# Sums of four v tokens by an accumulating load instead of TensorE, in a new instruction list with the stores on SyncE

## The chip, the cores and the metric

One core of a Trainium2 chip. The time is device time in microseconds (us) from the core's first to its last work, as the median of several executions. Executions of one kernel agree within 1 to 2%; a run more than 1.5% above the fastest of its kernel is called slow and left out of the ratios. In a trace, PE is TensorE, DVE is VectorE, ACT is ScalarE, POOL is GpSimd and SP is SyncE; a `q` behind a name is that engine's DMA issue. "L359" is a line of the kernel that the trace belongs to, so the same statement has another number in each kernel.

## The reference, cut to what matters

```python
# q, k, v: (8 batches, 8 heads, 576 tokens, 64), float32
q_d = q.reshape(B, H, 144, 4, D).mean(axis=3)      # means of 4 tokens
k_d = k.reshape(B, H, 144, 4, D).mean(axis=3)
v_d = v.reshape(B, H, 144, 4, D).mean(axis=3)
out_up = np.repeat(softmax_attention(q_d, k_d, v_d), 4, axis=2)
out_local = softmax_attention_within_3_tokens(q, k, v)     # banded mask
x = (out_up + out_local).transpose(0, 2, 1, 3).reshape(4608, 512)
out = elu(x @ w_in) @ w_out                                # 512 -> 2048 -> 512
```

The change touches only how `v_d` is formed for batches 3 to 7.

## The kernel before

The kernel handles heads in pairs (`j` = 0 to 3) and the tokens of the second part in nine blocks of 512. All instructions of all engines stand in one long list of words, `ORDER`, which was tuned; each engine executes its own instructions in the order of the list. `Cv3.0` is the cast of v of batch 3, pair 0 to fp16, `VD3.0` the copy of its four-token means out of PSUM, `mm1.2.5` one 128-row piece of the first matrix product for block 2, and `e`, `m`, `g` are the three steps of the ELU that TensorE's second product needs.

```python
def vsum_mm(b, j, to):                   # means of 4 tokens, by TensorE
    v16 = stV[(b, j)][0]
    for c in range(NB):                  # NB = 6
        nc.tensor.matmul(
            to[0:KG, c // 3, :],
            at_once("VR")[:, 48 - 24 * (c % 3) : 120 - 24 * (c % 3)], v16[:, c, :, :],
            start=(c % 3 == 0), stop=(c % 3 == 2),
        )

def turn(n, b, j):                       # words Tq, Tk
    ...
    if n == "q":
        vsum_mm(b, j, to[:, :, GW : GW + 128])

def v_away(b, j):                        # word VD
    x = tp[("v", b, j)] if nines(b) else tp[("q", b, j)][:, :, GW : GW + 128]
    vd = sb.tile([KG, 2, 128], FP16, tag="vd", bufs=7, name="vd")
    nc.vector.tensor_copy(out=vd[:], in_=x[0:KG])          # PSUM -> SBUF

def cast_v(b, j):                        # word Cv; cast_qk is alike
    nc.gpsimd.tensor_copy(out=t[:], in_=st32.pop(("v", b, j)).rearrange(...))

def x_add(b, j, t):                      # word X: local + global part, on GpSimd
    eng = nc.vector if (b, j, t) in X_DVE else nc.gpsimd
    eng.tensor_tensor(out=xts[t][...], in0=ln[:, a:z], in1=_rep4(...), op=AB.add)

def masked(b, j):                        # word M: two SBUF inputs
    nc.vector.tensor_tensor(out=mex[:], in0=pex[:], in1=mk2, op=AB.mult)

def elu_min(t, fc):                      # word m: SBUF to SBUF, fp16
    nc.vector.tensor_scalar(out=e[:], in0=e[:], scalar1=1.0, scalar2=-1.0, op0=AB.min, op1=AB.add)

def elu_add(t, fc):                      # word g: reads PSUM; TensorE waits for gt
    nc.vector.scalar_tensor_tensor(out=gts[t][:, fc, :], in0=hps[(t, fc)][:], scalar=0.0,
                                   op0=AB.max, in1=els.pop((t, fc))[:], op1=AB.add)

def store(t, tt):
    nc.scalar.dma_start(out=out[r : r + 128, :], in_=oss.pop((t, tt))[:])
```

The softmax here doesn't subtract the row's maximum and nothing guards it: scores larger than these inputs give would overflow.

Of the kernel before, what the change touches and what calls it, by code (L numbers as in the profile page):

```python
# [36 lines left out]
X_DVE, K_DVE = ((0, 3, 0),), ((0, 0), (0, 1))  # L37
ORDER = """
KM Lq0.0 KV TBL Lk0.0 FILL Lq0.1 KN Lk0.1 KE Lq0.2 KI Lk0.2 Cq0.0 Ck0.0 Lq0.3 Tq0.0 Lk0.3 Aq0.0
Tk0.0 Cq0.1 Lv0.0 Ak0.0 Ck0.1 Lv0.1 Z1 Tq0.1 Fq0.0 Lv0.2 SL0.0 Cq0.2 Aq0.1 Lv0.3 Fk0.0 Ck0.2  # L40
Tk0.1 G00.0 Z1 Tq0.2 Ak0.1 Cq0.3 G10.0 Fq0.1 Aq0.2 SD0.0 Ck0.3 Tk0.2 H00.0 Fk0.1 H10.0 KS Ak0.2
M0.0 SL0.1 Z2 Tq0.3 G00.1 Fq0.2 Cv0.0 G10.1 Fk0.2 Aq0.3 SD0.1 M0.1 Tk0.3 H00.1 H10.1 Fq0.3 Cv0.1
Ak0.3 SL0.2 Z1 VS0.0 Dq1.0 Fk0.3 G00.2 G10.2 VD0.0 WI0 SD0.2 WI1 Z2 VS0.1 H00.2 H10.2 Cv0.2
SL0.3 VD0.1 M0.2 G00.3 Z3 VS0.2 G10.3 Dk1.0 M0.3 SD0.3 OUT0.0 H00.3 VD0.2 WI2 H10.3 LG0.0 Z1
DEN0 WI3 WLv1.0 OUT0.1 Cv0.3 Lv1.0 RC0 Lv1.1 LG0.1 Lv1.2 VS0.3 RB0.0 Lv1.3 VD0.3 MUL0.0 RB0.1 Z1
OUT0.2 MUL0.1 X0.0.0 OUT0.3 LG0.2 X0.0.1 LG0.3 RB0.2 X0.1.1 X0.1.0 MUL0.2 Z1 RB0.3 Q0 MUL0.3
X0.2.1 X0.2.0 Q1 X0.3.0 Dk1.1 Q2 Dq1.1 mm1.0.0 mm1.0.2 e.0.0 X0.3.1 Tq1.1 WO0 Tk1.1 e.0.2 m.0.0
mm1.0.1 g.0.0 Ak1.1 WO1 mm1.0.3 Aq1.1 m.0.2 mm1.0.6 Fk1.1 WO2 e.0.3 Fq1.1 e.0.1 Tq1.0 Dk2.0
Tk1.0 Aq1.0 m.0.3 m.0.1 Ak1.0 g.0.1 WO3 SC1.1 Fq1.0 WLv2.0 Dq2.0 Lv2.0 mm1.0.7 Fk1.0 E01.1 Lv2.1
Cv1.0 Lv2.2 g.0.3 E11.1 Lv2.3 g.0.2 VS1.0 Lq3.0 mm1.0.11 VD1.0 e.0.7 M1.1 mm1.0.13 e.0.6 m.0.7  # L50
e.0.11 g.0.7 SC1.0 m.0.6 e.0.13 mm1.0.5 m.0.11 g.0.11 E01.0 m.0.13 mm1.0.9 E11.0 g.0.13 g.0.6
Tq1.2 Tk1.2 M1.0 Aq1.2 mm1.0.14 Ak1.2 Lk3.0 Cv1.1 Fq1.2 OUT1.0 e.0.5 Fk1.2 mm1.0.4 e.0.9 m.0.5
LG1.0 g.0.5 Tq1.3 e.0.4 Dq2.1 m.0.9 VS1.1 g.0.9 Aq1.3 mm2.0.0 VD1.1 e.0.14 Fq1.3 Tk1.3 OUT1.1
Ak1.3 Dk2.1 m.0.4 g.0.4 LG1.1 Fk1.3 SC1.2 m.0.14 g.0.14 mm2.0.1 E01.2 mm1.0.12 E11.2 mm1.0.8
e.0.12 M1.2 SC1.3 Lv3.0 m.0.12 e.0.8 g.0.12 Cv1.2 E01.3 m.0.8 mm1.0.10 g.0.8 E11.3 VS1.2 e.0.10
mm1.0.15 M1.3 VD1.2 DEN1 e.0.15 m.0.10 g.0.10 OUT1.2 m.0.15 mm2.0.2 RC1 LG1.2 g.0.15 RB1.1 RB1.0
MUL1.1 mm2.0.3 MUL1.0 X1.1.1 RB1.2 oc.0.0 MUL1.2 X1.0.2 mm2.0.4 X1.1.2 X1.0.1 Tq2.1 st.0.0 Tk2.1
Aq2.1 Cv1.3 mm2.0.5 Ak2.1 Fq2.1 X1.2.1 VS1.3 Fk2.1 Tq2.2 X1.2.2 mm2.0.6 Aq2.2 VD1.3 OUT1.3 Fq2.2
RB1.3 LG1.3 mm2.0.7 MUL1.3 Tk2.2 oc.0.1 mm2.0.8 Cv2.0 Lq3.1 Ak2.2 mm2.0.9 X1.3.2 Fk2.2 X1.3.1
mm2.0.10 st.0.1 Cv2.1 mm2.0.11 VS2.0 oc.0.2 mm2.0.12 Cv2.2 Lk3.1 VD2.0 SC2.1 mm2.0.13 E02.1  # L60
mm2.0.14 E12.1 Cv2.3 Lv3.1 mm2.0.15 M2.1 Tq2.0 oc.0.3 Cq3.0 Lq3.2 Tk2.0 Aq2.0 mm1.1.0 Ak2.0
Fq2.0 mm1.1.2 e.1.0 Ck3.0 Lk3.2 Fk2.0 SC2.2 e.1.2 m.1.0 g.1.0 E02.2 m.1.2 mm1.1.4 Lv3.2 g.1.2
Cv3.0 E12.2 Lq3.3 Tq2.3 e.1.4 M2.2 mm1.1.1 Aq2.3 Lk3.3 m.1.4 VS2.3 st.0.3 g.1.4 Cq3.1 Tk2.3
e.1.1 VD2.3 mm1.1.3 Ak2.3 m.1.1 Lv3.3 g.1.1 Ck3.1 SC2.0 e.1.3 Fk2.3 mm1.1.7 E02.0 m.1.3 g.1.3
E12.0 VS2.2 Fq2.3 Cv3.1 Lq4.0 mm1.1.5 e.1.7 VD2.2 M2.0 SC2.3 e.1.5 m.1.7 mm2.1.0 Lk4.0 E02.3
g.1.7 m.1.5 E12.3 mm1.1.6 g.1.5 Lv4.0 VS2.1 M2.3 e.1.6 mm1.1.8 VD2.1 m.1.6 DEN2 e.1.8 g.1.6
Cv3.2 Lq4.1 OUT2.1 RC2 mm1.1.9 LG2.1 m.1.8 g.1.8 RB2.1 st.0.2 OUT2.3 e.1.9 MUL2.1 mm1.1.10 LG2.3
m.1.9 RB2.3 g.1.9 X2.1.3 e.1.10 OUT2.0 X2.1.2 MUL2.3 mm1.1.11 LG2.0 m.1.10 RB2.0 g.1.10 X2.3.2
e.1.11 mm2.1.1 MUL2.0 Cv3.3 mm1.1.12 m.1.11 g.1.11 X2.0.3 OUT2.2 e.1.12 X2.0.2 RB2.2 LG2.2
mm1.1.14 m.1.12 g.1.12 X2.3.3 Tq3.0 e.1.14 MUL2.2 mm1.1.13 Aq3.0 Cq3.2 Tk3.0 m.1.14 e.1.13 Lk4.1  # L70
mm2.1.2 VD3.0 X2.2.2 Ak3.0 g.1.14 Tq3.2 Ck3.2 KD3.0 mm1.1.15 m.1.13 Aq3.2 Lv4.1 g.1.13 Cv4.0
Lq4.2 Tk3.2 e.1.15 VD3.2 X2.2.3 mm1.2.0 Ak3.2 m.1.15 g.1.15 Tq3.1 e.2.0 KD3.2 mm2.1.3 Aq3.1
Cq3.3 Tk3.1 m.2.0 oc.1.0 Lk4.2 mm1.2.2 VD3.1 Cq4.1 Ak3.1 g.2.0 Ck4.0 mm2.1.4 st.1.0 KD3.1 e.2.2
Ck3.3 SC3.1 mm1.2.12 m.2.2 E03.1 Lv4.2 g.2.2 Cv4.1 Lq4.3 mm2.1.5 E13.1 mm1.2.1 e.2.12 M3.1 SC3.0
m.2.12 e.2.1 g.2.12 mm2.1.6 E03.0 m.2.1 g.2.1 mm1.2.10 E13.0 Cv4.2 Tq3.3 e.2.10 Tk3.3 M3.0 Aq3.3
mm1.2.15 m.2.10 Ak3.3 g.2.10 Cq4.0 mm2.1.7 e.2.15 VD3.3 Lk4.3 KD3.3 mm2.1.8 m.2.15 oc.1.1 Lv4.3
g.2.15 st.1.1 SC3.3 Lq5.0 Lk5.0 mm2.1.9 E03.3 mm2.1.10 E13.3 mm1.2.5 M3.3 SC3.2 e.2.5 mm1.2.6
E03.2 m.2.5 g.2.5 mm2.1.11 E13.2 Tq4.0 e.2.6 M3.2 oc.1.2 Tk4.0 m.2.6 mm2.1.12 st.1.2 g.2.6 Ck4.2
Ak4.0 DEN3 Aq4.0 Ck4.1 KD4.0 mm2.1.13 VD4.0 Lv5.0 RC3 Lq5.1 mm2.1.14 SO3 mm2.1.15 Tq4.1 oc.1.3
Tk4.1 st.1.3 Cq4.2 mm1.2.3 Aq4.1 Cq5.0 Ak4.1 Lk5.1 mm1.2.7 VD4.1 Lv5.1 e.2.3 KD4.1 Tq4.2 Lq5.2  # L80
e.2.7 m.2.3 g.2.3 Tk4.2 SI3 Cq4.3 mm2.2.0 m.2.7 g.2.7 Ck4.3 Aq4.2 Lk5.2 mm1.2.9 Ak4.2 Ck5.0
VD4.2 Lv5.2 mm1.2.4 e.2.9 KD4.2 m.2.9 SC4.2 e.2.4 g.2.9 E04.2 m.2.4 mm1.2.11 g.2.4 E14.2
mm1.2.13 e.2.11 M4.2 SC4.1 e.2.13 m.2.11 mm2.2.1 g.2.11 E04.1 m.2.13 mm1.2.8 E14.1 g.2.13
mm1.2.14 e.2.8 M4.1 m.2.8 SC4.0 e.2.14 g.2.8 E04.0 m.2.14 mm2.2.2 g.2.14 E14.0 OUT3.0 mm2.2.3
MUL3.0 Cv4.3 OUT3.1 oc.2.0 M4.0 Lq5.3 OUT3.3 st.2.0 Lk5.3 MUL3.1 X3.0.3 mm2.2.4 Lv5.3 X3.0.4
MUL3.3 mm2.2.5 X3.1.3 mm2.2.6 X3.3.4 X3.1.4 OUT3.2 X3.3.3 Tq4.3 MUL3.2 Cv5.1 mm2.2.7 Aq4.3
X3.2.3 Tk4.3 VD4.3 oc.2.1 mm2.2.8 Ck5.2 Ak4.3 mm1.3.0 st.2.1 X3.2.4 KD4.3 Cv5.0 SC4.3 e.3.0
mm1.3.3 Cv5.2 E04.3 Lq6.0 m.3.0 mm2.2.9 E14.3 g.3.0 Tq5.0 e.3.3 M4.3 mm1.3.7 Aq5.0 m.3.3 g.3.3
Cq5.1 DEN4 e.3.7 VD5.0 Cq5.3 Lk6.0 mm1.3.6 RC4 m.3.7 Tk5.0 SO4 g.3.7 Tq5.1 e.3.6 Ck5.1 Ak5.0
mm1.3.5 m.3.6 Aq5.1 Lv6.0 g.3.6 Cq5.2 mm2.2.10 Lq6.1 e.3.5 KD5.0 VD5.1 Lk6.1 mm1.3.1 m.3.5 Lv6.1  # L90
g.3.5 Lq6.2 Tk5.1 e.3.1 mm1.3.8 Lk6.2 Ak5.1 m.3.1 g.3.1 mm2.2.11 SI4 KD5.1 mm1.3.11 e.3.8 SC5.1
oc.2.2 m.3.8 g.3.8 e.3.11 mm2.2.12 E05.1 m.3.11 g.3.11 mm1.3.10 E15.1 mm1.3.9 e.3.10 M5.1 st.2.2
SC5.0 m.3.10 e.3.9 mm2.2.13 g.3.10 E05.0 m.3.9 mm1.3.13 g.3.9 E15.0 mm1.3.4 e.3.13 M5.0 Tq5.2
m.3.13 e.3.4 g.3.13 Tk5.2 Aq5.2 mm2.2.14 m.3.4 g.3.4 Ck5.3 Ak5.2 mm1.3.2 VD5.2 Ck6.0 Lv6.2 KD5.2
mm2.2.15 e.3.2 m.3.2 OUT4.2 oc.2.3 g.3.2 OUT4.0 st.2.3 MUL4.2 mm1.3.14 Cv5.3 mm2.3.0 MUL4.0
e.3.14 X4.2.4 Lq6.3 X4.2.5 OUT4.1 OUT4.3 m.3.14 MUL4.1 X4.0.5 mm2.3.1 X4.0.4 MUL4.3 mm1.3.12
X4.1.5 g.3.14 Tq5.3 e.3.12 X4.3.4 Tk5.3 X4.1.4 Aq5.3 mm1.3.15 m.3.12 Ak5.3 g.3.12 Cq6.1 mm2.3.2
e.3.15 VD5.3 X4.3.5 KD5.3 mm1.4.0 m.3.15 g.3.15 Ck6.2 SC5.3 e.4.0 Cq6.2 mm1.4.5 E05.3 m.4.0
mm2.3.3 E15.3 g.4.0 Cv6.1 mm2.3.4 e.4.5 Cv6.0 oc.3.0 Tq6.1 M5.3 st.3.0 mm1.4.9 m.4.5 Aq6.1 g.4.5
Cq6.0 mm2.3.5 VD6.1 e.4.9 Cv6.2 Lk6.3 mm1.4.1 Lv6.3 m.4.9 g.4.9 Lq7.0 SC5.2 e.4.1 Lk7.0 mm1.4.7  # L100
E05.2 m.4.1 g.4.1 mm2.3.6 E15.2 Tq6.0 e.4.7 M5.2 mm1.4.8 Aq6.0 m.4.7 g.4.7 DEN5 e.4.8 VD6.0
m.4.8 mm1.4.6 RC5 g.4.8 Tq6.2 SO5 e.4.6 Tk6.0 Cq6.3 Aq6.2 mm1.4.2 Ak6.0 m.4.6 mm2.3.7 g.4.6
Cq7.0 e.4.2 KD6.0 Ck6.1 mm1.4.15 VD6.2 oc.3.1 st.3.1 m.4.2 mm2.3.8 Lv7.0 e.4.15 g.4.2 Lq7.1 SI5
m.4.15 mm2.3.9 Lk7.1 g.4.15 Lv7.1 Tk6.1 Lq7.2 mm1.4.3 Ak6.1 Tk6.2 KD6.1 e.4.3 mm2.3.10 Ck7.0
Lk7.2 Ak6.2 mm1.4.11 m.4.3 g.4.3 Ck6.3 mm2.3.11 KD6.2 e.4.11 Lv7.2 m.4.11 SC6.1 oc.3.2 g.4.11
mm1.4.12 E06.1 mm2.4.0 E16.1 mm1.4.4 e.4.12 M6.1 SC6.0 m.4.12 e.4.4 g.4.12 mm2.3.12 st.3.2 m.4.4
E06.0 g.4.4 mm1.4.13 E16.0 mm2.4.1 e.4.13 M6.0 OUT5.3 m.4.13 OUT5.2 MUL5.3 mm1.4.10 MUL5.2
mm2.3.13 X5.3.6 e.4.10 g.4.13 X5.3.5 mm2.3.14 X5.2.5 m.4.10 mm2.3.15 g.4.10 X5.2.6 OUT5.1 oc.3.3
OUT5.0 MUL5.1 Cv7.1 st.3.3 mm1.4.14 Cv6.3 MUL5.0 mm2.4.2 e.4.14 X5.1.5 Lq7.3 X5.0.5 Tq6.3 Lk7.3
m.4.14 Tk6.3 Lv7.3 g.4.14 X5.1.6 Aq6.3 mm1.5.0 Ak6.3 Cv7.0 VD6.3 mm1.5.5 e.5.0 KD6.3 X5.0.6  # L110
SC6.3 e.5.5 m.5.0 mm2.4.3 g.5.0 Cq7.1 E06.3 m.5.5 mm1.5.10 E16.3 g.5.5 Cv7.2 Tq7.0 oc.4.0 M6.3
# [73 lines left out]
def kernel(  # L185
# [92 lines left out]
    def nines(b):  # L278
        return b in NINES
# [481 lines left out]
```

## Time and profile before

| | before |
|---|---|
| time | 368.07 us (two runs, 366.47 and 369.66) |
| span of the profiled run, granted clock | 367.9 us, 0.986 |
| busy: PE, DVE, ACT, POOL | 96%, 65%, 57%, 33% |
| chain that ended last | PE 76%, DMA 8%, ACT 5%, DVE 3% |
| TensorE holes and slow starts: to 80 us, 80 to 260 us, after 260 us | 25.3, 12.0, 1.9 us |

The last row is worked out from the trace: for each pair of neighbouring matmuls, the time from start to start minus what is usual (the median) for that shape in the same trace, where the excess is over 0.05 us. It is the time that TensorE lost. The prediction shows the page's lines. Two groups that it does not show will matter later, both on VectorE (the number before the comma is us in total, after it the mean ns of one):

```profile
L664 DVE TENSOR_SCALAR e<-e 128x512 f16<-128x512 f16 x144 | 51.5, 359 | 48.9 <-ACT e L660 48.1
...
L521 DVE TENSOR_TENSOR mex<-pex,MASK 112x1152 f16<-112x1152 f16 x32 | 25.7, 802 | 13.8 <-ACT pex L502 13.7
```

An undisturbed `e` step takes 0.28 us and an undisturbed mask product 0.75. The means, 0.359 and 0.802, are higher: some of these steps are stretched already in the kernel before.

### The profile page before, as it was taken

To read this page: it belongs to the slowest core of one execution; us is meant where nothing else is said; L and a number is where in the kernel's file an instruction comes from. 1 tells how busy PE (TensorE), PEld (TensorE's weight loads), DVE (VectorE), ACT (ScalarE), POOL (GpSimd) and SP (SyncE) were. 2 spreads that over 40 slices of the span, in tenths; PEclk is the share of its full clock that TensorE was granted. 3 is DMA by queue.
4 is the path that set the end of the run, shared out by engine and by line. 5 is a ranking of instruction groups with operands and counts; after the bars stand their busy time and mean duration, and the time that the engine had idled before them with its cause. 6 is when DMAs were issued, how large, how long until landed. Compare 5 with 4: busy or idle time off the path is not lost.

```text
span 367.9 us, 9507 instructions
## 1 busy us (share of the span) xinstructions
PE 351.5 (96%) x3953; PEld 183.8 (50%) x3953; DVE 239.7 (65%) x472; ACT 208.4 (57%) x395; POOL 120.4 (33%) x177
## 2 busy tenths in 40 slices
PE   7888989899999999999999999999999999999996
PEld 3554454444555565554555545564544444444442
DVE  2856986429897548777797667887674765565520
ACT  2844883448768768377657564768363334344321
POOL 6676224361175122562292308410500410000000
PEclk9998999699999999999999999999999999999999
DMA  7999999999839959499649861112104010010012
GB/s 265 206 201 198 197 197 192 196 199 196 137 74 229 166 126 193 95 182 180 140 112 199 192 118 56 41 47 68 59 32 110 29 60 29 29 59 29 29 59 86
DMA packets 106917, 46.08 MB, mean 125 GB/s; under 512 B 92314, under 2 KB 101178, under 8 KB 106874
## 3 DMA queue, kind: packets, MB, share of 16 engines
q1 hardware_dynamic: 91402, 25.17, 40.2%
q10 hardware_dynamic: 8896, 13.36, 12.3%
q0 software_dynamic: 6576, 6.94, 11.0%
q8 instruction: 31, 0.51, 0.6%
q14 instruction: 12, 0.10, 0.1%
HBM read 42.49 MB, written 9.53 MB: 141 GB/s over the span
## 4 chain that ended last, share of the span: by engine, by line
PE 76%; DMA 8%; ACT 5%; DVE 3%; issue 3%; SPq 2%; ACTq 1%; POOL 1%; POOLq 0%
PE op L679 32%; PE hp L635 28%; DMA v<-in_v_dram 7%; PE lg L584 3%; PE sc L476 2%; SPq L316 2%; DVE gt L669 2%; PE den L539 2%; ACT e L660 2%; PE tq L369 1%; PE tq L392 1%; PE tk L392 1%; DVE e L664 1%; DMA q<-in_q_dram 1%; PE lg L590 1%
## 5 line engine op out<-in xcount | busy, mean ns | idle before, releaser
L635 PE MATMUL hp<-xt,WI 128*128 128x512 f16 x576 | 143.7, 381 | 2.3 <-DVE gt L669 2.0
L679 PE MATMUL op<-WO,gt 128*128 128x512 f16 x576 | 142.0, 384 | 0.4 <-DVE gt L669 0.3
L660 ACT ACTIVATE e<-hp 128x512 f16<-128x512 f32 x144 | 85.9, 601 | 76.0 <-PE hp L635 70.4
L669 DVE SCALAR_TENSOR_TENSOR gt<-hp,e 128x512 f16<-128x512 f32 x144 | 99.2, 690 | 4.7
L679 PEld LDWEIGHTS <-gt 128*128 128x128 f16 x576 | 53.6, 98 | 63.1 <-issue 1.8
L635 PEld LDWEIGHTS <-WI 128*128 128x128 f16 x576 | 53.3, 98 | 61.7 <-issue 5.0
L664 DVE TENSOR_SCALAR e<-e 128x512 f16<-128x512 f16 x144 | 51.5, 359 | 48.9 <-ACT e L660 48.1
L627 POOL TENSOR_TENSOR xt<-ln,gn 128x64 f16<-128x64 f16 (+7 forms) x63 | 41.8, 685 | 68.1 <-DVE ln L614 67.7
L686 ACT COPY os<-op 128x512 f32<-128x512 f32 x36 | 21.1, 587 | 41.9 <-PE op L679 41.8
L502 ACT ACTIVATE pex<-sc 112x576 f16<-112x576 f32 x64 | 41.0, 648 | 5.5 <-PE sc L486 4.2
L359 POOL CAST v<-v 112x768 f16<-112x768 f32 x30 | 24.8, 838 | 40.8 <-PE lg L584 22.7
L521 DVE TENSOR_TENSOR mex<-pex,MASK 112x1152 f16<-112x1152 f16 x32 | 25.7, 802 | 13.8 <-ACT pex L502 13.7
L354 POOL CAST q<-q 96x768 f16<-96x768 f32 x20 | 16.8, 842 | 31.0 <-issue 21.2
L508 ACT ACTIVATE dex<-sc 72x288 f16<-72x288 f32 x64 | 25.5, 405 | 1.5 <-PE sc L486 1.5
L354 POOL CAST k<-k 96x768 f16<-96x768 f32 x20 | 17.4, 876 | 26.3 <-PE tk L392 20.6
L417 ACT CAST qt<-tq 128x720 f16<-128x720 f32 x20 | 15.2, 761 | 11.5 <-PE tq L369 7.9
L476 PEld LDWEIGHTS <-kt 64*112 64x112 f16 x384 | 13.1, 127 | 14.0 <-issue 10.0
L476 PE MATMUL sc<-qt,kt 64*112 64x96 f16 x384 | 16.9, 217 | 2.1 <-ACT kt L412 0.6
L369 PEld LDWEIGHTS <-VR 112*72 112x72 f16 x192 | 13.0, 113 | 7.2 <-ACT qt L412 2.9
L614 DVE TENSOR_TENSOR ln<-lg,rcb 128x576 f16<-128x576 f32 x20 | 15.0, 748 | 0.0
L584 PEld LDWEIGHTS <-v 112*64 112x64 f16 x384 | 10.4, 111 | 7.8 <-issue 5.7
L450 DVE CAST vd<-tq 72x256 f16<-72x256 f32 x20 | 8.3, 415 | 8.8 <-ACT qt L417 8.7
(64 smaller groups left out, 273.8 us busy)
## 6 DMA issues: line engine op xcount, KB each, us to landing
v<-in_v_dram SPq DMA_DIRECT2D x28, 336.0 KB, 7.3
out_dram<-os ACTq DMA_DIRECT2D x36, 256.0 KB, 2.5
q<-in_q_dram SPq DMA_DIRECT2D x24, 288.0 KB, 5.1
k<-in_k_dram SPq DMA_DIRECT2D x24, 288.0 KB, 6.5
rcb<-rd ACTq DMA_DIRECT2D x10, 360.0 KB, 5.2
WI<-in_moe_w_in_dram POOLq DMA_DIRECT2D x4, 512.0 KB, 11.5
WO<-in_moe_w_out_dram POOLq DMA_DIRECT2D x4, 512.0 KB, 16.8
q<-in_q_dram POOLq DMA_DIRECT2D x4, 288.0 KB, 11.1
```

The source lines that it names most:

```text
L354: nc.gpsimd.tensor_copy(out=t, in_=x.rearrange("p (e c d) -> p c e d", e=2, d=D))
L359: nc.gpsimd.tensor_copy(out=t[:], in_=st32.pop(("v", b, j)).rearrange("p (e c) d -> p c e d", e=2))
L476: nc.tensor.matmul(sc[e][0:KW, c // 3, QB * (c % 3) : QB * (c % 3) + QB], kt[r, QB * c : QB * c + KW], q_of(b, j, r, c), start=True, stop= ...
L502: nc.scalar.activation(out=stS[(b, j)][2][:, e, :].rearrange("p (g u) -> p g u", g=2), in_=scs[(b, j)][e][0:KW, :, 0:HB], func=AF.Exp, sca ...
L508: nc.scalar.activation(out=stS[(b, j)][1][:, e], in_=scs[(b, j)][e][0:KG, :, HB : HB + SD], func=AF.Exp, scale=SCALE / 16.0,)
L521: nc.vector.tensor_tensor(out=mex[:], in0=pex[:], in1=mk2, op=AB.mult)
L627: eng.tensor_tensor(out=xts[t][:, j, t0 - TBLK * t : t1 - TBLK * t], in0=ln[:, a:z], in1=_rep4(gn[:, a // 4 : z // 4]), op=AB.add,)
L635: nc.tensor.matmul(hps[(t, fc)][:], WI[:, dc, 128 * fc : 128 * fc + 128], xts[t][:, dc, :], start=(dc == 0), stop=(dc == DMC - 1),)
L660: nc.scalar.activation(out=e[:], in_=hps[(t, fc)][:], func=AF.Exp)
L664: nc.vector.tensor_scalar(out=e[:], in0=e[:], scalar1=1.0, scalar2=-1.0, op0=AB.min, op1=AB.add)
L669: nc.vector.scalar_tensor_tensor(out=gts[t][:, fc, :], in0=hps[(t, fc)][:], scalar=0.0, op0=AB.max, in1=els.pop((t, fc))[:], op1=AB.add,)
L679: nc.tensor.matmul(ops[(t, tt)][:], gts[t][:, fc, 128 * tt : 128 * tt + 128], WO[:, fc, :], start=(fc == 0), stop=(fc == FCN - 1),)
```

## The change

TensorE is the bound, so work is taken from it. For batches 3 to 7, v is loaded a second time: GpSimd's DMA brings tokens 0 and 1 of each group of four (word U), then adds tokens 2 and 3 onto them during the transfer (word V), and VectorE adds the remaining two numbers. The sums are not divided by four; instead the denominators use an indicator of 4.0. Stores go from ScalarE to SyncE, and the list is a new one.

```diff
+V4, STORE_SP = (3, 4, 5, 6, 7), True
 ORDER = """
 ... (all words in a new order, with U and V words for batches 3 to 7)
+    ind[:, 52:104] = 4.0 * ind[:, 0:52]
+    def wide():
+        return sb.tile([128, 2 * RW], FP32, tag="lg32", bufs=2, name="lg32")
+
+    def load_v4(h, b, i):
+        if not h:
+            t = wide()[0:KG, 0:1024].rearrange("p (g h d) -> p g h d", h=2, d=D)
+            ...
+        a = v[b, 4 * i]
+        nc.gpsimd.dma_start(
+            out=st4[(b, i, "all")],
+            in_=bass.AP(tensor=a.tensor, offset=a.offset + 2 * D * h,
+                        ap=[[4 * D, KG], [4 * D * KG, 8], [D, 2], [1, D]]),
+            **({"accum_op": AB.add} if h else {}),
+        )
-        if n == "q":
+        if n == "q" and b not in V4:
             vsum_mm(b, j, to[:, :, GW : GW + 128])
     def v_away(b, j):
+        if b in V4:
+            vd = sb.tile([KG, 4, D], FP16, tag="vd", bufs=7, name="vd")
+            x = st4.pop((b, j))
+            nc.vector.tensor_tensor(out=vd[:], in0=x[:, :, 0], in1=x[:, :, 1], op=AB.add)
+            ...
+            return
 ... (denominators and OUT index the new tiles)
-        nc.scalar.dma_start(out=out[r : r + 128, :], in_=oss.pop((t, tt))[:])
+        eng = nc.sync if STORE_SP else nc.scalar
+        eng.dma_start(out=out[r : r + 128, :], in_=oss.pop((t, tt))[:])
```

## The prediction

> **What bounds the kernel now.** I read the busy shares first, then the slices over time, then the chain of waits, then the waits of single engines and single stretches. The page's totals and slices:
>
> ```profile
> PE 351.5 (96%) x3953; PEld 183.8 (50%) x3953; DVE 239.7 (65%) x472; ACT 208.4 (57%) x395; POOL 120.4 (33%) x177
> ...
> PE   7888989899999999999999999999999999999996
> ...
> DMA  7999999999839959499649861112104010010012
> GB/s 265 206 201 198 197 197 192 196 199 196 137 74 229 166 126 193 95 182 180 140 112 199 192 118 56 41 47 68 59 32 110 29 60 29 29 59 29 29 59 86
> ```
>
> One slice is 9.2 us. Two regimes show. For about the first eight slices PE has holes while the DMA engines are full at about 200 GB/s: there the kernel waits for weights and for the inputs of batches 0 to 2. After some 75 us PE is at 9 in every slice to the end, and no other engine is. The cut of the span into stretches says the same: PE is busy for 49.4 of the 50 us from 100 on, 49.7 of the next 50, 50.0 of the next and 49.9 of the next. The chain that ended last gives 76% to PE and 8% to DMA. So after 75 us a microsecond of PE work removed is a microsecond gained, unless a new wait takes it; before that the loads set the pace.
>
> Two PE groups are nearly everything, and one small group is what the change touches:
>
> ```profile
> L635 PE MATMUL hp<-xt,WI 128*128 128x512 f16 x576 | 143.7, 381 | 2.3 <-DVE gt L669 2.0
> L679 PE MATMUL op<-WO,gt 128*128 128x512 f16 x576 | 142.0, 384 | 0.4 <-DVE gt L669 0.3
> ...
> L369 PE MATMUL tq<-v,VR 112*72 112x128 f16 x120 | 10.0, 219 | 0.0
> ...
> L450 DVE CAST vd<-tq 72x256 f16<-72x256 f32 x20 | 8.3, 415 | 8.8 <-ACT qt L417 8.7
> ```
>
> A mean of 219 ns is the latency of one pipelined matmul, not its price. The price is read from starts in the order of time:
>
> ```profile
> 243.32 0.48 PE L392 MATMUL tq<-I,q 96*128 96x120 f16 x6
> 243.64 0.50 PE L369 MATMUL tq<-v,VR 112*72 112x128 f16 x6
> 243.97 0.48 PE L392 MATMUL tk<-I,k 96*128 96x120 f16 x6
> ```
>
> Six token-sum matmuls occupy PE from 243.64 to 243.97, some 0.33 us. Measured over all 20 such sixes in the trace, from first start to the start of what follows, it is 0.336 us each, without spread.
>
> **A wait that the stores cause.** In the crowded head there is one visible PE hole of 2.4 us, and the timeline there names it:
>
> ```profile
> 60.36 0.59 ACT L686 COPY os<-op 128x512 f32<-128x512 f32 x1 [1.75 <-PE op L679]
> 63.11 2.17 SPq L306 DMA_DIRECT2D q<-in_q_dram  x1
> 64.86 0.38 ACTq L690 DMA_DIRECT2D out_dram<-os  x1
> 65.28 0.64 ACT L412 CAST qt<-tq 128x576 f16<-128x576 f32 x1 [4.34 <-DMA v<-in_v_dram]
> 65.98 0.53 PE L369 MATMUL vs<-v,VR 112*72 112x128 f16 x6 [2.41 <-ACT qt L412]
> ```
>
> The output copy ended at 60.95, yet ACT's store was issued at 64.86; SyncE's own load issues took 1.8 to 6.2 us each in that stretch. ACT stood for 4.3 us with a ready cast behind the store, and PE for 2.4. The profile blames a load of v; I read it as ACT waiting to issue. All other stores are issued within some 0.03 us of their copy's end (or a little before it) and hold ACT for about 0.34 us.
>
> **What the skill says.** The Trainium skill, "TensorE: Matmul & The Clock Gate", section "Wait — 56ns, not 53.3ns?", gives 55.6 ns from start to start for 128 columns on the full clock; the trace has a median of 55 ns inside a six, so it agrees. "Perfetto Trace Analysis", section "DMA Instruction — HWDGE (DVE, Sync)", says that the descriptor generator is shared and locked for exclusive use by one issuer; the 4.3 us above fit that. "DMA: Bandwidth & Descriptors", section "SWDGE vs HWDGE vs iDMA", says that only GpSimd's path can accumulate. No run here yet shows an accumulating DMA, so its time is my largest unknown. "SBUF — State Buffer", section "SBUF: two separate sides", says that a VectorE instruction with two SBUF inputs and a GpSimd instruction that reads SBUF exclude each other; the new additions of v are such instructions, and before's trace gives no separate number for it.
>
> **The change, part by part.**
>
> *Removed from PE:* batches 3 to 7 have 5 x 4 = 20 head pairs; each loses six matmuls. 20 x 0.336 = 6.7 us, all of it after 75 us where PE is dense. The instruction order agrees: 240 PE rows fewer, which is 120 weight loads and 120 matmuls. Nothing replaces them on PE: the denominators use a second copy of the indicator with 4.0 because the sums are no longer means, with as many matmuls. Two side gains, not counted apart: the transposed q no longer needs the v cast, and the PSUM pair is free after ACT's cast, where VectorE's read of vd used to follow it (8.7 us of VectorE's idle time ended by that cast).
>
> *VectorE:* 20 PSUM casts of 415 ns become 20 additions of 256 float32. The multiplies here take 303 ns for 144 elements and 748 ns for 576, so about 1.03 ns an element, which puts 256 elements at 418 ns: no change.
>
> *GpSimd:* 20 more DMA issues. Those in the page take 0.71 to 0.77 us, so about 15 us more on 120, beside PE. GpSimd must wait in its queue for the first half to land before it issues the accumulating half.
>
> *DMA:* each of the 20 moves 72 x 8 runs of 512 B, 295 KB; 5.9 MB in all on 46.1 MB. The load queue's packets average 275 B and 25.9 ns, the software queue's 1055 B and 98 ns, so 512 B is about 50 ns. 576 x 50 / 16 = 1.8 us a DMA, 36 us for all, while batches 3 to 7 pass (before: some 110 to 260 us). The mean use there is well under full, but single slices reach 9.
>
> *Moved:* 36 stores leave ACT (about 0.34 us each, 12 us of a 57% busy engine, worth nothing by itself after 75 us) and join SyncE's queue behind loads. The wait shown above should vanish: about 2.4 us. The new list leaves PE's order unchanged until the first half of the MLP's start; after that it interleaves differently, with one v load postponed behind the second weight matrix.
>
> Sum: -6.7 for PE, about -2 for the store wait (some of the hole may reopen for data), and an allowance of +1.5 for new waits, chosen from the next part: -7.2, from 368.1 to 361.
>
> **Rivals.** (1) *The accumulated v lands late.* By the PE work between the words in the new list at dense rates, batches 3 and 4 leave 5.8 to 8.2 us from the first half's issue to the second's and mostly 7 to 8 us from that to VectorE's addition; later batches leave 12 to 28. Before's software loads took 11 us in the full head and plain v loads 7.3. If the accumulate takes 9 us, VectorE stands, the ELU behind it stands, and PE with it: up to 2 us at four places, 364 to 367 us. For it: tight gaps exactly where DMA is still busy. Against: only four transfers are tight. (2) *Stores stuck in SyncE's queue.* SyncE waits a lot for staging buffers (casts on GpSimd end about 93 us of its waits after 70 us, up to 9.2 us, or 15.7 for the last v, at once). A store behind such a load is late, and with two output buffers the copy after next stands. The list leaves 10 us or more between a copy and the copy after next through batch 7, so I give it 1 us; at worst 3 to 4, for 364 us. (3) *DMA becomes the bound.* Extra traffic delays q, k and v loads. Ten staging buffers give nearly a batch of lead, so only local delays; at worst time stays at 368. (4) *The better outcome:* the head also loses the half-clock stretch at 61 to 68 us that goes with the hole, and the freed PSUM helps: 356 to 358.
>
> **Range and chances.** The sure term alone gives 361.4, and gains and losses around it are of like size. I take 361.0, with 355.5 to 367.0 for 8 in 10. The 2% line is at 360.7, almost my middle; because before's two runs differ by 3.2 us and new waits are likelier than new windfalls, I put faster at 0.44, within 2% at 0.52, slower at 0.04.
>
> **What would show it.** Right: 20 x 6 matmuls of the sum gone, PE's busy slices unbroken after 75 us, no ACT cast waiting some 4 us behind a store, VectorE's additions at about 420 ns and rarely waiting for a DMA. Wrong: VectorE waiting on the accumulated v in batches 3 and 4, ACT's output copy waiting for a store, GpSimd waiting long between the halves with casts late behind it, or new PE holes before 75 us from the new list.

## The result, and the profile after

The changed kernel is correct and takes 384.52 us (382.57 and 386.48) against 368.07. Ratios here and below are those over fast runs of the same rounds, so they are not quite the ratio of the medians quoted. This one is 1.046 (95% interval 1.033 to 1.058): slower by some 4.5%, where a gain of 2% was forecast. Even the upper end of the range, 367.0, was far off.

The page of the changed kernel, totals and slices (one slice is now 9.5 us):

```profile
PE 349.6 (92%) x3833; PEld 178.5 (47%) x3833; DVE 252.2 (66%) x472; ACT 206.9 (54%) x395; POOL 145.1 (38%) x197
...
PE   7898989989966998889988999999999999999996
...
PEclk9988999989998999999999999999999999999999
```

The 120 matmuls are gone (3953 became 3833). But where before every slice after 75 us was a 9, there are now 6s and 8s between about 105 and 210 us (slices 12 to 22). The granted clock (PEclk) is at 8 in slice 13, right behind two TensorE holes that the timeline below shows. The chain that ended last has only 67% PE, and 15% DVE instead of 3%. The groups show who waits for whom (last fields: idle time of the engine just before the group, and what ended most of it):

```profile
L666 PE MATMUL hp<-xt,WI 128*128 128x512 f16 x576 | 144.7, 387 | 12.2 <-DVE gt L700 11.7
L710 PE MATMUL op<-WO,gt 128*128 128x512 f16 x576 | 138.9, 380 | 3.4 <-DVE gt L700 3.3
...
L549 DVE TENSOR_TENSOR mex<-pex,MASK 112x1152 f16<-112x1152 f16 x32 | 32.2, 1006 | 22.2 <-ACT pex L530 21.9
...
L359 POOL DMA_DIRECT2D lg<-in_v_dram x20 | 23.2, 1214 | 34.0 <-DMA lg<-in_v_dram 22.7
...
L376 POOL CAST q<-q 96x768 f16<-96x768 f32 x20 | 20.5, 1032 | 12.8 <-PE tq L414 7.6
...
L473 DVE TENSOR_TENSOR vd<-lg 72x256 f16<-72x256 f32 x20 | 15.1, 764 | 0.0
```

TensorE waited 15.0 us for VectorE's `gt` in these two groups; before it was 2.3. The addition of v, forecast at 418 ns, takes 764 on average, though its undisturbed ones take 410: it is stretched, like the mask product (1006 after 802). GpSimd's casts of q went from 842 to 1032 ns by their records, but records of neighbours on GpSimd overlap here, as the timeline below shows, so this is not all lost time. And GpSimd stood 22.7 us waiting for first halves to land. VectorE's wait for the landing of the second halves, the prediction's first rival, is absent: idle time before L473 is 0.0.

| TensorE holes and slow starts | to 80 us | 80 to 260 us | after 260 us |
|---|---|---|---|
| before | 25.3 | 12.0 | 1.9 |
| changed | 21.2 | 35.1 | 2.0 |

So the head gained 4.1 us, and the stretch of batches 3 to 7 lost 23.1. Less the 6.7 us of work taken away this makes +12.4 us, and the two profiled spans differ by 12.9 (380.8 and 367.9). The granted clock has a small share in it: (1 - clock) times the span is 5 us before (0.986) and 7 us for the changed kernel's profiled run (0.982), but 12 us for its other run (0.969). Whether holes bring the lower clock was not tested.

The timeline of the changed kernel at its worst place, in the order of time (start, duration, engine, then in brackets the idle time before it and its releaser):

```profile
108.48 2.11 POOL L658 TENSOR_TENSOR xt<-ln,gn 128x192 f16<-128x192 f16 x3
108.67 2.90 DVE L695 TENSOR_SCALAR e<-e 128x512 f16<-128x512 f16 x1 [0.24 <-ACT e L691]
...
110.55 0.86 POOL L359 DMA_DIRECT2D lg<-in_v_dram  x1
...
111.40 0.84 POOL L376 CAST k<-k 96x768 f16<-96x768 f32 x1
...
112.20 1.43 POOL L359 DMA_DIRECT2D lg<-in_v_dram  x1
...
112.34 1.02 PE L666 MATMUL hp<-xt,WI 128*128 128x512 f16 x4 [2.91 <-DVE gt L700]
...
113.05 2.17 POOL L381 CAST v<-v 112x768 f16<-112x768 f32 x2
113.13 3.65 DVE L549 TENSOR_TENSOR mex<-pex,MASK 112x1152 f16<-112x1152 f16 x1
...
117.76 1.86 PE L666 MATMUL hp<-xt,WI 128*128 128x512 f16 x4 [2.90 <-DVE gt L700]
```

GpSimd ran here without a gap: each instruction starts where the one before ends, or, from the accumulating issue on, some 0.6 us before the end on record. VectorE's `e` step, 0.28 us when alone, took 2.90, through two more additions of x and a DMA issue; the mask product took 3.65 instead of 0.75. Behind them the ELU's gate `gt` was late, and TensorE stood twice for 2.9 us. Note also the second of the two DMA issues, the accumulating one: 1.43 us, where the plain one took 0.86.

**Theories.** A *shut-out* is a VectorE step that lasts far longer than its usual duration while GpSimd's instructions run; it is called long where the step passes the ends of three or more of them. S: long shut-outs of VectorE by gapless GpSimd runs cost the time. Loads: the issues, the waits for landings and the accumulation cost it, with or without shut-outs. List: the new order leaves too little slack. Stores: SyncE holds stores behind waiting loads.

### The profile page after: what moved, and what is told of

It reads as the page before. It is cut to its first block, busy times and chain, and to the rows that moved or that the text cites. A ratio compares the mean times of both kernels' runs of the same rounds, so it can differ in the third digit from the quotient of the medians.

```text
span 380.8 us, 9345 instructions
## 1 busy us (share of the span) xinstructions
PE 349.6 (92%) x3833; PEld 178.5 (47%) x3833; DVE 252.2 (66%) x472; ACT 206.9 (54%) x395; POOL 145.1 (38%) x197
## 3 DMA queue, kind: packets, MB, share of 16 engines
q10 hardware_dynamic: 3712, 3.93, 4.7%
## 4 chain that ended last, share of the span: by engine, by line
PE 67%; DVE 15%; DMA 8%; ACT 4%; issue 2%; ACTq 1%; POOL 1%; SPq 0%; DVEq 0%
PE op L710 28%; PE hp L666 26%; DVE gt L700 5%; DMA rd<-rc 4%; DVE e L695 3%; DVE mex L549 3%; PE lg L613 3%; DMA v<-in_v_dram 3%; PE sc L504 2%; ACT e L691 2%; PE den L568 1%; DMA q<-in_q_dram 1%; PE rb L602 1%; ACT pex L530 1%; DVE ln L645 1%
## 5 line engine op out<-in xcount | busy, mean ns | idle before, releaser
L666 PE MATMUL hp<-xt,WI 128*128 128x512 f16 x576 | 144.7, 387 | 12.2 <-DVE gt L700 11.7
L710 PE MATMUL op<-WO,gt 128*128 128x512 f16 x576 | 138.9, 380 | 3.4 <-DVE gt L700 3.3
L666 PEld LDWEIGHTS <-WI 128*128 128x128 f16 x576 | 54.5, 99 | 76.6 <-issue 20.7
L695 DVE TENSOR_SCALAR e<-e 128x512 f16<-128x512 f16 x144 | 52.7, 367 | 54.3 <-ACT e L691 53.3
L549 DVE TENSOR_TENSOR mex<-pex,MASK 112x1152 f16<-112x1152 f16 x32 | 32.2, 1006 | 22.2 <-ACT pex L530 21.9
L359 POOL DMA_DIRECT2D lg<-in_v_dram x20 | 23.2, 1214 | 34.0 <-DMA lg<-in_v_dram 22.7
L381 POOL CAST v<-v 112x768 f16<-112x768 f32 x30 | 28.1, 961 | 17.7 <-PE lg L613 9.0
L376 POOL CAST k<-k 96x768 f16<-96x768 f32 x20 | 19.1, 956 | 16.9 <-issue 9.4
L376 POOL CAST q<-q 96x768 f16<-96x768 f32 x20 | 20.5, 1032 | 12.8 <-PE tq L414 7.6
L442 ACT CAST kt<-tk 128x576 f16<-128x576 f32 x20 | 13.0, 651 | 4.7 <-PE hp L666 2.8
L473 DVE TENSOR_TENSOR vd<-lg 72x256 f16<-72x256 f32 x20 | 15.1, 764 | 0.0
```

The source lines that it names most:

```text
L376: nc.gpsimd.tensor_copy(out=t, in_=x.rearrange("p (e c d) -> p c e d", e=2, d=D))
L666: nc.tensor.matmul(hps[(t, fc)][:], WI[:, dc, 128 * fc : 128 * fc + 128], xts[t][:, dc, :], start=(dc == 0), stop=(dc == DMC - 1),)
L710: nc.tensor.matmul(ops[(t, tt)][:], gts[t][:, fc, 128 * tt : 128 * tt + 128], WO[:, fc, :], start=(fc == 0), stop=(fc == FCN - 1),)
```

## The experiments

Eighteen kernels ran. Names begin with n (new list, nothing else), a or t (changed kernel) or o (old list). Where a part was taken away, the result is sometimes wrong. The texts were written before each run and name their theories in their own words.

### First: one part at a time

**n_list**: the new list and SyncE stores, but the sums back on TensorE, no second load, `VD` right after ScalarE's copy of q.

```diff
-V4, STORE_SP = (3, 4, 5, 6, 7), True
+V4, STORE_SP = (), True     # and no U, V words in ORDER
```

> The new list and the stores by SyncE, but with the token sums back on TensorE in all batches (no loads of v by GpSimd; each copy of the sums right behind the copy of q). Theory G (the software DMAs on GpSimd and the dense GpSimd runs they make shut VectorE out of SBUF, which costs the changed kernel some 20 us in batches 3 to 7): with them gone, VectorE's mask products and ELU steps are of their old lengths (mean under 850 and 375 ns) and the time is 360 to 371 us, near the kernel before. Theory L (the new list itself is bad: casts and copies just in time): 378 us or more, since the list is kept and 6.7 us of TensorE work comes back.

Measured: 385.41 us, ratio 1.051 (1.045 to 1.057). The new list is slow even without any new load. VectorE's steps have about their old lengths (mask product 807 ns, `e` 366), with one long shut-out (3.83 us). It is not a clean measure of the list, for the list was made for a TensorE without the sums, and the place of `VD` costs some 2 us of waits for PSUM of its own; but a list that is neutral is excluded.

**a_st_act**: the changed kernel with stores on ScalarE (`STORE_SP = False`).

> The changed kernel with the stores issued by ACT again. Theory S (stores wait behind loads in SyncE's queue and hold back output copies or loads): 374 us or less. Theories G and L: 382 to 388 us, with the ACT wait of about 4 us behind a store at 60 to 66 us back in the trace.

Measured: 392.78 us, ratio 1.071 (1.063 to 1.080), above both ranges. Stores on SyncE are not to blame: taking them away made the changed kernel 8 to 9 us slower, and the rival Stores falls. That the stores themselves make this difference is not shown: ScalarE's wait of 4 us behind a store did not come back, while the trace has two new things: VectorE stood 5.20 us for an accumulated v that landed late (160.73 us), with a TensorE wait of 6.48 us behind it, and an addition of v was shut out for 5.12 us (257.98 us), with a TensorE wait of 2.76 behind it.

**a_plainv**: the second half overwrites instead of being added (wrong).

```diff
-            **({"accum_op": AB.add} if h else {}),
+            **({}),
```

> The changed kernel with the second half loaded plainly over the first (a wrong result on purpose: the sums miss tokens 0 and 1), so the same DMAs, waits and lists without the accumulation. If accumulating is what costs (theory A: 1.38 us of GpSimd per issue in place of 0.86, and a slower landing): the issues fall to about 0.87 us, the casts behind them to 0.84 us, and the time to 372 to 378 us. If any software DMA there costs alike, the time stays at 381 to 386 us.

Measured: 377.19 us, ratio 1.031 (1.023 to 1.038). With as many transfers and bytes but no addition, GpSimd's issues of L359 fell from a mean of 1.21 us to 0.83 and its casts of q from 1.03 to 0.90. Accumulation costs some 5 to 7 us here, though the two intervals overlap.

**o_dummy**: the kernel before with the 20 GpSimd loads of the change, which nobody reads, at the same progress of TensorE. Everything else is as before, except that two wide buffers, which the loads share, stand for four narrow ones of the same tag; correct.

> The kernel before with its old list and its stores on ACT, plus the same 20 GpSimd loads of v (10 plain, 10 accumulating) at the same progress of TensorE, which nothing reads. Theory G or plain DMA traffic: 376 to 388 us with stretched VectorE instructions (longest over 2 us). Theory L or S: 367 to 371 us, as the additions alone would be harmless.

Measured: 386.05 us, ratio 1.053 (1.047 to 1.059). Twenty loads that add no work to TensorE or VectorE cost the old list some 20 us. Its trace has four long shut-outs, the worst a VectorE `e` step of 5.23 us at 241 us with a TensorE hole of 3.7 us behind it.

### Second: without loads, and the old list without sums

**a_nouv**: the changed kernel without any second load; the additions read a constant tile (wrong).

```diff
     def load_v4(h, b, i):
-        ...                       # both DMAs
+        # a zero tile, set once, for all batches
```

> The changed kernel without any of the 20 GpSimd loads: VectorE's 20 additions read a constant tile (a wrong result on purpose), list and stores as changed, TensorE 6.7 us lighter. If the loads are the whole loss (theory G): 357 to 363 us. If the new list itself is slow, as the 385.4 us of it with the sums on TensorE suggests (theory L): 374 to 380 us. In between, both count.

Measured: 374.56 us, ratio 1.020 (1.013 to 1.027); its profiled run is slow (377.63). TensorE has the 6.7 us less, there is no second load, and still the kernel is slower than before. The longest VectorE step in that slow run is an addition of 4.39 us.

**a_uonly**: only the ten plain first halves are loaded (wrong): `if h: return` before the DMA.

> The changed kernel with the ten plain first halves alone, none of the ten accumulating ones (a wrong result on purpose): half the packets, no GpSimd wait between halves. Plainly overwriting gave 377.2 us with all 20. If each software DMA costs alike: halfway between the run without loads and 377.2. If the waits of GpSimd for a first half to land make the loss: within 2 us of the run without loads.

Measured: 379.34 us, ratio 1.039 (1.030 to 1.048), no less than a_plainv with twice the transfers, and near neither of the two expected values. The number of plain transfers is not what counts. Nor is GpSimd's wait for first halves to land: a_plainv has it (17.4 us in all), a_uonly does not, and a_plainv is no slower.

**o_st_sp**: the kernel before with stores on SyncE, nothing else; correct.

> The kernel before with its stores issued by SyncE, nothing else. My prediction's term: 362 to 366 us (the 4 us wait of ACT behind the first store goes). If stores hold back loads in SyncE's queue: 368 us or more.

Measured: 365.12 us, ratio 0.997 (0.990 to 1.004). The ScalarE wait of 4.3 us that the prediction read is gone in this trace. In its place an output copy waited 6.0 us for the landing of an earlier store (copy at 72.58 us): the prediction's second rival. In all, the move is worth next to nothing in the old list.

**o_nosum**: the old list, stores by ScalarE, no sums on TensorE from batch 3 on, VectorE additions of a constant tile instead of PSUM casts (wrong).

```diff
-        if n == "q":
-            vsum_mm(b, j, to[:, :, GW : GW + 128])
+        # v_away from batch 3 on:
+            nc.vector.tensor_tensor(out=vd[:], in0=x[:, :, 0], in1=x[:, :, 1], op=AB.add)
```

> The old list and stores on ACT, batches 3 to 7 without the 120 sum matmuls, and 20 VectorE additions of a constant tile at the places of the old casts (a wrong result on purpose). It is the term of 6.7 us alone: 357 to 362 us if TensorE work removed is time gained, 363 to 367 if something else takes its place at once.

Measured: 369.62 us, ratio 1.010 (1.004 to 1.016). This is above both expected ranges. Here the term that the prediction called sure stands alone, and it did not come. At 102.6 us an `e` step took 4.20 us, with a TensorE hole of 4.1 us behind it.

### Third: is it the long steps?

**o_novd**: o_nosum without the additions too (a constant result tile; wrong).

> The kernel before, old list, stores by ScalarE; the sums of v on TensorE are left out from batch 3 on and NO VectorE step takes their place (a constant zero tile is used, so the result is wrong on purpose). The run with VectorE additions of a constant tile in place of the sums took 369.6, 3.5 us more than before. Theory S2 (the two-input SBUF addition, open to the shut-out where the old PSUM cast was not, ate the gain): about 359 to 361, the whole 6.7 us of TensorE work gained. Rival T (any shift of the tuned timing brings a shut-out or a half-clock stretch somewhere): 364 or more, with a stretched step of over 2 us or a half-clock stretch in the trace although the additions are gone.

Measured: 367.32 us, ratio 1.001 (0.992 to 1.009). The additions were not the culprit; a long shut-out is there without them, as rival T had it. The timeline shows why nothing was gained:

```profile
106.42 0.82 POOL L354 CAST q<-q 96x768 f16<-96x768 f32 x1 [1.20 <-issue]
...
106.90 4.33 DVE L671 TENSOR_SCALAR e<-e 128x512 f16<-128x512 f16 x1
...
107.45 0.84 POOL L634 TENSOR_TENSOR xt<-ln,gn 128x384 f16<-128x384 f16 x1
...
108.24 0.82 POOL L354 CAST k<-k 96x768 f16<-96x768 f32 x1
...
109.01 0.83 POOL L359 CAST v<-v 112x768 f16<-112x768 f32 x1
...
109.80 0.52 POOL L634 TENSOR_TENSOR xt<-ln,gn 128x192 f16<-128x192 f16 x1
...
110.25 0.82 POOL L354 CAST q<-q 96x768 f16<-96x768 f32 x1
```

A step of 0.28 us was shut out by a run of GpSimd instructions and ended just after the last of them. It outlasted seven, one a short memset that is left out above, so it did not go on at the first six ends. TensorE's hole behind it was 3.4 us.

**t_enop, o_enop, o_nosum_enop**: the changed kernel, the kernel before, and o_nosum, each with an empty engine instruction after every GpSimd cast and addition of x from batch 2 on.

```diff
+    def pause(b):
+        if b >= 2:
+            nc.gpsimd.engine_nop()
```

> The changed kernel with one edit: after each GpSimd cast and each GpSimd addition of x (from batch 2 on) an empty engine instruction is put on GpSimd, which reads and writes nothing. Results stay right. Theory S (VectorE's steps with two SBUF inputs or at double rate are shut out for several gapless GpSimd instructions in a row, because it misses the moments between them): the empty instruction opens a gap between GpSimd's instructions, no VectorE step passes more than one end of a GpSimd instruction (changed kernel: 9 passed two or more, up to 3.65 us), and the time falls from 384.5 to about 372 to 378. Rival L (the late loads and the list's order cost the time, the stretched steps only accompany it): within 2 us of 384.5, or worse by the empty instructions' own time.

> The kernel before with the same empty GpSimd instructions. Theory S: the kernel before has no step that passes three or more ends, only some 6 us of shorter stretches beside a dense TensorE, so at most 3 us are gained: 362 to 366. Rival (the empty instructions delay GpSimd's casts and cost by themselves): 368 or more; then the run of the changed kernel with them has to be read against this one.

> The kernel before without sums on TensorE from batch 3 on, with two-input VectorE additions of a constant tile (wrong on purpose; 369.6 without the pauses), and the empty GpSimd instructions added. Theory S: the 4.2 us step at 102 us and its TensorE hole go, and the 6.7 us appear: 359 to 362. Rival T or L: 367 to 371.

Measured: t_enop 378.78 us, ratio 1.030 (1.020 to 1.040; its profiled run is slow); o_enop 367.32, ratio 1.001 (0.992 to 1.010); o_nosum_enop 363.69, ratio 0.991 (0.984 to 0.999). The edit did not do what it was for: GpSimd's instructions, which overlapped by 0.03 to 0.05 us, still overlap by some 0.02. In t_enop long shut-outs remain (3.87 us at 110.8, 3.93 at 165.8), so its gain cannot be put down to their absence and it tests nothing. The other two lie above what theory S had asked for. The third is telling by its trace: no step was stretched by more than 1.4 us there, and of the three old-list kernels without sums it is the one that gained.

**t_sem, o_sem**: a real gap. The empty instruction raises a semaphore and GpSimd's next instruction waits for it.

```diff
+            nc.gpsimd.engine_nop().then_inc(apart, 1)
+            nc.gpsimd.wait_ge(apart, count[0])
```

> The changed kernel; after each GpSimd cast and addition of x from batch 2 on an empty GpSimd instruction raises a semaphore, and GpSimd's next instruction waits for it. Unlike the empty instruction alone, which left the next one starting 0.02 us before the last one's end, this must open a real gap (some 0.05 to 0.3 us) at each of about 120 places. Results stay right. Theory S (long shut-outs of VectorE cost the time): no VectorE step passes three or more ends of GpSimd instructions where the gaps are, and the time falls to 368 to 376. Rival L (list and late loads): 378 or more, as GpSimd only becomes later.

> The kernel before with the same semaphore gaps on GpSimd. Theory S: 362 to 366, as its steps are stretched by one GpSimd instruction at most and could now start in the gaps. Rival (gaps delay the casts that TensorE needs): 369 or more.

Measured: t_sem 379.53 us, ratio 1.034 (1.028 to 1.039); o_sem 368.82, ratio 1.005 (1.001 to 1.009). Now GpSimd's casts and additions are mostly 0.10 to 0.17 us from what follows them, and this is the same place of the list as above:

```profile
110.78 0.51 POOL L668 TENSOR_TENSOR xt<-ln,gn 128x192 f16<-128x192 f16 x1 [0.17 <-POOLq L373]
111.45 2.36 POOL L668 TENSOR_TENSOR xt<-ln,gn 128x384 f16<-128x384 f16 x2
...
111.96 0.95 DVE L559 TENSOR_TENSOR mex<-pex,MASK 112x1152 f16<-112x1152 f16 x1 [0.42 <-ACT pex L540]
112.83 0.28 DVE L707 TENSOR_SCALAR e<-e 128x512 f16<-128x512 f16 x1
```

The long shut-outs are gone in all six kernels with this edit (here and below): the largest excess of any VectorE step in them is 1.4 us. In one, o_nosum_sem, a step still passed three short ends, with an excess of under 0.8 us, at 20 us, before the gaps begin. The table counts, in each profiled run, VectorE's stretched steps that passed three or more ends of GpSimd instructions, and gives the largest excess of a step over its usual duration.

| kernel | steps that passed 3 or more | largest excess, us | ratio |
|---|---|---|---|
| before | 0 | 1.0 | |
| changed | 5 | 3.3 | 1.046 |
| n_list | 1 | 3.6 | 1.051 |
| o_dummy | 4 | 5.0 | 1.053 |
| a_nouv (slow run) | 2 | 4.0 | 1.020 |
| a_st_act | 7 | 4.7 | 1.071 |
| a_plainv, a_uonly | 4, 4 | 3.3, 3.3 | 1.031, 1.039 |
| t_enop (slow run) | 5 | 3.6 | 1.030 |
| o_st_sp, o_enop | 1, 0 | 1.0, 1.3 | 0.997, 1.001 |
| o_nosum, o_novd | 1, 2 | 3.9, 4.0 | 1.010, 1.001 |
| o_nosum_enop | 0 | 1.4 | 0.991 |
| t_sem, o_sem | 0, 0 | 1.2, 0.7 | 1.034, 1.005 |

The count does not order the ratios: a_plainv with four, t_enop with five and t_sem with none are at 1.030 to 1.034. And theory S as it was put, 368 to 376 us for t_sem, falls: with all long shut-outs gone, the changed kernel is still 3.4% slower than before. They are at most a part of its loss, and the smaller one. In the old list without sums they are more than that: o_nosum lost all of its gain, and the runs without long shut-outs (o_nosum_enop, and o_nosum_sem below) have a good part of it.

### Fourth: a square of list and loads, free of long shut-outs

All with the semaphore gaps, no sums on TensorE from batch 3 on, VectorE additions, and SyncE stores. **o_real_sem** is the whole change in the old list, with `U`, `V` and `VD` at the progress of TensorE that they have in the new one (correct); **a_nouv_sem** is a_nouv with gaps, **o_nosum_sem** is o_nosum with gaps and SyncE stores (both wrong). t_sem is the fourth corner.

> The whole change (loads with accumulation, VectorE additions, no sums on TensorE, stores by SyncE) in the OLD list, the loads and additions put in at the same TensorE progress as in the new list, with the semaphore gaps on GpSimd. Correct. Together with the next two runs and the changed kernel with gaps (379.5, ratio 1.034) it makes a square of list and loads, all without long shut-outs. Theory list (the new order of words is what leaves VectorE, ScalarE and TensorE too little slack): 364 to 369. Theory loads (late landings and longer GpSimd issues make the holes in either list): 374 to 382.

> The changed kernel without any GpSimd load of v (additions read a constant tile, wrong on purpose) with the semaphore gaps. Without gaps it took 374.6 (ratio 1.020) with one shut-out of 4.4 us. Theory list: 368 to 373, still above the kernel before although TensorE has 6.7 us less. Theory loads: 361 to 365.

> The fourth corner: the old list without sums and without loads, additions of a constant tile (wrong on purpose), stores by SyncE, gaps. Without gaps and with ScalarE stores 369.6; with the weaker empty instructions 363.7. If the shut-outs ate the 6.7 us here: 359 to 363. If not: 366 or more.

| | no second load | loads with accumulation |
|---|---|---|
| old list | o_nosum_sem: 362.44 us, 0.988 (0.985 to 0.992) | o_real_sem: 382.68 us, 1.043 (1.039 to 1.047) |
| new list | a_nouv_sem: 370.72 us, 1.011 (1.007 to 1.015) | t_sem: 379.53 us, 1.034 (1.028 to 1.039) |

TensorE's holes between 80 and 260 us in the same square: 16.0 and 33.9 us in the old list, 21.2 and 31.5 in the new. Neither pure theory holds. Loads add 5.5 points (20 us) to the old list and 2.3 points (8 us) to the new one; the new list, read without loads, costs 2.3 points (8 us) more than the old one, and saves some of that back when the loads are there, perhaps because it was made for them. That o_nosum_sem comes to 0.988 shows that TensorE's term was real: some 4 us of the 6.7 arrive once the long shut-outs are out of the way. The gaps and SyncE stores do not make this gain: o_st_sp_sem, below, has both with the sums kept, and is at 0.999 (0.995 to 1.002).

How loads cost time without any long shut-out is seen in the waits. In o_real_sem the first rival of the prediction happened:

```profile
119.88 0.25 PE L513 MATMUL sc<-qt,kt 64*112 64x96 f16 x1
123.18 0.76 DVE L482 TENSOR_TENSOR vd<-lg 72x256 f16<-72x256 f32 x2 [5.91 <-DMA lg<-in_v_dram]
...
124.78 0.30 DVE L469 CAST kd<-tk 128x144 f16<-128x144 f32 x1
125.00 0.28 DVE L706 TENSOR_SCALAR e<-e 128x512 f16<-128x512 f16 x1
125.13 0.71 PE L513 MATMUL sc<-qt,kt 64*112 64x96 f16 x11 [5.00 <-DVE kd L469]
```

VectorE stood 5.91 us for the accumulated v, and with it `kd`, and TensorE for 5.00. VectorE waits 11.7 us for such landings in this run, and GpSimd 42.5 us (six waits, the longest 12.7) for first halves. In the new list (t_sem) VectorE waits only 1.9 us, and GpSimd less too:

```profile
POOL lg L359 <- DMA lg<-in_v_dram: 23.6, 6, 8.2
```

These 23.6 us (six waits, the longest 8.2) hold up every cast behind them. What that costs TensorE is small: it waits 3.2 us in t_sem for casts of q and k (0.3 in a_nouv_sem) and 11.1 us for `gt` (7.6). The two differences, 2.9 and 3.5 us, compare with the 10.3 us of holes by which t_sem exceeds a_nouv_sem between 80 and 260 us; the rest is spread over many small holes and is not resolved. How the loads cost their time in the new list is thus shown only in part.

**o_st_sp_sem**: an attempt to beat both kernels with what had helped, the kernel before with SyncE stores and gaps (correct).

> A version meant to beat both kernels, correct: the kernel before with stores by SyncE (365.1, ratio 0.997) and the gaps. If the gaps' cost seen in the kernel before (ratio 1.005) was its half-clock stretches and not the gaps themselves: 361 to 364. Otherwise 365 to 368, no gain.

Measured: 366.98 us, ratio 0.999 (0.995 to 1.002). No gain. No correct version here beats the kernel before by more than its own spread.

## Why the prediction was wrong, point by point

- **The bound** was read rightly: TensorE after 75 us. The 240 rows went, and without long shut-outs (o_nosum_sem against before, 1 - 0.988) the gain is 1.2%, some 4.3 us. The forecast of 6.7 was the right work, but "a microsecond of PE work removed is a microsecond gained" was too strong.
- **The store wait** came out as said for the head: holes before 80 us fell by 4.1 us where about 2 were forecast, and no ScalarE cast waits behind a store any more. As a gain by itself it failed: o_st_sp is at 0.997, and its interval (0.990 to 1.004) holds 1. Two readings beside it were wrong. Not all other stores follow their copy within 0.03 us: seven come 0.1 to 15.5 us later, as the list puts other words between. And the half-clock stretch lies at 67 to 74 us of the span, not at 61 to 68.
- **The failed step is the allowance of +1.5 us for new waits.** The prediction took the waits that the new loads, the additions and the new list would bring between 80 and 260 us for 1.5 us; the trace shows 23 us more of TensorE holes there, over half of it before matmuls that wait for VectorE's `gt` (15.0 us instead of 2.3). Taking the ratios of the runs one after the other, on some 367 us (a point is 1% of the time before): from before to o_nosum_sem -1.2 points, -4.3 us; the new list +2.3 points, +8.4 us; the loads +2.3 points, +8.2 us; the long shut-outs, from t_sem to the changed kernel, +1.2 points, +4.4 us. The sum, +16.7 us, is the 4.6% measured by construction, since each step starts where the last one ends; the sizes of the steps are what the runs tell. The order of the steps matters (loads alone cost 20 us in the old list), and the last step is the least certain, as the two intervals overlap and t_enop came to 1.030 with long shut-outs still in its (slow) trace; it rests as well on a_nouv, which gained 0.9 points by gaps, and on o_nosum, which gained 2.1 with gaps and SyncE stores, of which SyncE stores are worth 0.3.
- **"VectorE: no change" (418 ns) failed** by its mean, 764 ns. The cost of the step itself was right: 14 of the 20 took 0.41 us. What failed is that nothing would stretch it: six took 0.78 to 3.69 us. The prediction had quoted the rule that such an addition and a GpSimd instruction exclude each other, and said that the trace before gives no number for it. It did: the `e` steps at a mean of 359 ns against 280 undisturbed, 24 of them stretched by 10.3 us in sum.
- **"GpSimd beside PE, 15 us" failed.** The issues took 23.2 us, 1.21 us each, since the accumulating ones take about 1.4. Beside PE they are not: in gapless runs with the casts and additions they shut VectorE out, on which TensorE waits.
- **The rivals.** (1) named the right transfer, but put it at 2 us at four places; in the old list it gave one hole of 5.0 us (o_real_sem), with the stores on ScalarE one of 6.5 us (a_st_act); in the changed kernel itself VectorE does not wait for it, and GpSimd waits 22.7 us for first halves. (2) does occur in the old list, where an output copy waited 6.0 us (o_st_sp) and 4.0 us (o_real_sem) for a store, but not in the changed kernel, which is slower with its stores on ScalarE. (3) did not show: halving the plain transfers (a_uonly against a_plainv) gained nothing. The move of words, "interleaves differently", had been given no number at all, and it is one of the two largest terms.
- **Open:** why the new list without loads is 8 us slower than the old one. In the profiled runs, whose spans differ by 5.0 us, 5.2 us is seen as more holes between 80 and 260 us, in part as small waits for `gt` (7.6 against 4.5 us); what makes `gt` late was not traced. Why a shut-out lasts past some ends of GpSimd instructions and not past others is open too.

## What to carry to other kernels

An engine at 33% is not free: ask which of its neighbours share a resource with it, and look in the profile for steps whose mean is above their undisturbed duration before adding work there. Taking work from the bound pays only as far as the engines that feed it have slack at that place, so a list tuned for one set of durations has to be tested by itself, apart from the change that it carries. A tuned kernel is a special point: here several quite different shifts of its timing brought a VectorE step of over 4 us, which the tuned one did not have.

## What the Trainium skill lacked or had wrong

- "SBUF — State Buffer", section "SBUF: two separate sides", says that the shared port pair is held for a whole instruction and that the other engine blocks. Agreed as to which VectorE steps suffer: in all twenty traces only the fp16 `e` step, the mask product and the addition of v were stretched, never one that reads PSUM. Lacking: a blocked VectorE step can miss several ends of GpSimd instructions in a row when these leave no gap. A step of 0.28 us went on only at the seventh end, after 4.3 us (o_novd), and in o_dummy after 5.2 us; with gaps of mostly 0.10 to 0.17 us between GpSimd's instructions no step in six kernels had an excess above 1.4 us.
- "DMA: Bandwidth & Descriptors", section "SWDGE vs HWDGE vs iDMA", names accumulation as a feature of GpSimd's path and gives no cost. Here an accumulating issue is recorded with 1.4 us against 0.81 to 0.89 for a plain one of the same shape, and the change with plain loads in place of accumulating ones ran at 1.031 instead of 1.046.
- No page that I read has it: a GpSimd cast right behind an accumulating issue is mostly recorded with 1.36 to 1.41 us instead of 0.82, and starts some 0.55 us before the issue's recorded end. In a gapless run the overlap is handed on (casts that start at 113.05, 113.82 and 114.58 us, 0.77 us apart, each recorded with 1.40), so the two long records are not to be added: an issue and its cast took 2.20 to 2.26 us from start to end against 1.65 with a plain issue (a_plainv).
- No page that I read has it: an empty engine instruction on GpSimd does not separate its neighbours (overlap of 0.02 us remains); one that raises a semaphore on which the next waits gives 0.14 us.
